# A written order for every engine through the first fourteen steps of an attention and feed-forward kernel, with the raw weights staged whole

## The chip, the cores and the metric

The kernel runs on one core of a Trainium2 chip. Five engines work side by side, each through its own list of instructions in order: TensorE (PE in the profile; its weight loads are PEld), VectorE (DVE), ScalarE (ACT), GpSimd (POOL) and SyncE (SP), which here only issues transfers. They meet through semaphores. The metric is the device time of one execution in microseconds (us); lower is better.

## The reference, cut to what matters

```python
# q, k, v: (4, 8, 768, 64); block = 32, window = 16, scale = 1/8, nb = 24
k_sum = k.reshape(B, H, nb, block, D).max(axis=3)        # 24 key summaries
v_sum = v.reshape(B, H, nb, block, D).mean(axis=3)       # 24 value summaries
scores_l = where(|i - j| < window, scale * q @ k.T, -1e9)
scores_s = scale * q @ k_sum.T + log(block)
a = softmax(concat(scores_l, scores_s), eps=1e-9)        # local keys, then summaries
x = a @ concat(v, v_sum)                                 # -> (3072, 512)
h = x @ w_in                                             # (3072, 2048)
g = (a0 + a1*h + a2*h*h + a3*h*h*h) / (1 + |b0|*|h| + |b1|*h*h + 1e-6)
out = g @ w_out                                          # (3072, 512)
```

The weights arrive as 64-bit floats and everything else as 32-bit ones.

## The kernel before, in words

**Attention** goes by "halves" of 64 queries, all eight heads at once; there are 48, twelve to a batch. A half sees 96 local keys and 24 summaries, so 120 columns for each of four head pairs. `att_a` makes the scores on PE, adds the mask and takes the row minimum on DVE (`tensor_tensor_reduce`, L195), the exponential with its row sum on ACT (L199), the small addition and the reciprocal on DVE (L201, L202), and scales the rows on POOL (L204). `att_b` turns the rows over on PE (L222) and copies them out of PSUM on ACT (L228). `att_c` multiplies with the values (for group 0 it also splits the result into a high and a low part, L252 and L253); `values` does two halves at once for the later groups.

**Feed-forward** goes by six groups of 512 tokens and sixteen chunks of 128 hidden columns: 96 steps. A step is twelve matmuls of the first layer (`moe1`), the rational function on ACT, DVE and POOL (`gelu`, L340 to L351), and, for the chunk three steps back (`LAG`), twelve matmuls of the second layer (`moe2`), with the transposes of a half between them. Three matmuls stand for one because each operand is split into a high and a low part.

**Weights.** Each of the sixteen chunks is loaded raw (1 MB), turned from a 64-bit float into a 32-bit one (ACT L314, POOL L316, DVE L317), copied as the high part (ACT L320) and subtracted for the low part (DVE L321). The first eight chunks come as one transfer each into a four-deep buffer; the last eight come as two transfers of 512 KB into the two-deep buffer `stage`, which the raw keys and values of later batches also use. `w_split` of chunk `fc` is traced five steps ahead (`CVL`).

**Start.** Group 0 needs its eight halves before the first step can begin. In that stage the kernel also makes the value summaries of batch 0 and of batch 1 by matmul (L154) and, where the planner puts them, splits of the first weight chunks.

**Order.** PE keeps the order of the text from the first step on (`chained`). DVE, ACT, POOL and the transfers are ordered by a planner that simulates a timeline and reads priorities (`high_priority`); only a few reductions on DVE are held in program order. `start_of` puts the halves of group 1 at steps 1, 2, 4, 5, 7, 8, 10 and 12.

Of the kernel before, what the change touches and what calls it, by code (L numbers as in the profile page):

```python
# [8 lines left out]
F32 = mybir.dt.float32  # L9
# [6 lines left out]
PSUM = bass.MemoryType.PSUM  # L16

# [25 lines left out]
CVL = 5  # L43
NEARLY = 3
SOFF = 12
VLAG = 5
NWARM = 6
FIRST = "Q0 K0 K1 V0 K2 K3 Q1 V1 S V2 W0 V3 F W1 V4 W2 G W3 V5"
AVGAT = 4
# [10 lines left out]
def tile_kernel(ctx, tc, qw_in, kraw, kwin, vpad, vred, wio, a, b, cmask, cident, cavg, out):  # L60
# [6 lines left out]
    wl = ctx.enter_context(tc.tile_pool(name="wl", bufs=NLATE))  # L67
# [7 lines left out]
    chained = []  # L75

    def mm(*args, **kw):
        ins = nc.tensor.matmul(*args, **kw)  # L78
        if chained:
            tc.keep_in_program_order(ins)  # L80
# [58 lines left out]
    def value_sum(bi, c):  # L139
        vs, vr = vsum[bi], sums.pop(("v", bi, c))  # L140
        tc.keep_in_program_order(nc.vector.tensor_reduce(vs[:, c, :], vr, axis=AX.X, op=ALU.add))
        if c == NVC - 1:
            nc.vector.tensor_scalar_mul(vs, vs, 1.0 / BLK)
# [9 lines left out]
    def value_average(bi, av, vt, i):  # L153
        nc.tensor.matmul(av[:NK, :], avg[:, AVGW - NK - 4 * i:AVGW - 4 * i], vt[i], start=(i == 0), stop=(i == len(vt) - 1))  # L154
        if i < len(vt) - 1:
            return
        if bi == 0:
            for i in range(2):
                nc.scalar.copy(vw[i][NKW:NK, :], av[NKW:NK, :])
            for t in vres[2:6]:  # L160
                nc.scalar.copy(t[NKW:NK, :], av[NKW:NK, :])
        else:
            t = gp.tile([NK, DM], F32, tag="gh", name="vn")
            nc.scalar.copy(t[NKW:NK, :], av[NKW:NK, :])
            nc.sync.dma_start(out=vnext, in_=t[NKW:NK, :])
# [9 lines left out]
    def att_a(jj, pool=None, tag="a", sbuf=None):  # L175
        bi, j = divmod(jj, NJ)
        kt, qt = kw[jj % 2], qw[jj % 2] if jj >= HPG else qres[:, jj]
        if j < 2 and bi > 0 or jj in (HPG, HPG + 1):
            nc.vector.tensor_copy(kt[:, NKC - 1], ksum[bi])
        mt = mask[:, 0 if j == 0 else (2 if j == NJ - 1 else 1), :]  # L180
        sc = (pool or ps_a).tile([P, 512], F32, tag=tag, name=f"sc{jj}")
        for pr in range(NPAIR):
            if jj >= HPG:
                parts = ((0, NK, kt[:, :, pr, :]),)
            else:
                parts = ((0, NKW, kres[:, pr, j * HQ:j * HQ + NKW]), (NKW, NK, ksum[0][:, pr, :]))
            for lo, hi, keys in parts:
                for e in range(2):
                    rows = slice(e * D, (e + 1) * D)
                    mm(sc[rows, pr * NK + lo:pr * NK + hi], qt[rows, pr, :], keys[rows], start=True, stop=True)  # L190
        sbuf, stag = sbuf or (pp, "p")
        ss = sbuf.tile([P, NPAIR, NK], F32, tag=stag, name=f"ss{jj}")
        sm = sp.tile([P, 2, NPAIR], F32, tag="sm", name=f"sm{jj}")
        for pr in range(NPAIR):
            nc.vector.tensor_tensor_reduce(  # L195
                out=ss[:, pr, :], in0=sc[:, pr * NK:(pr + 1) * NK], in1=mt, op0=ALU.add, op1=ALU.min,
                scale=-SCALE, scalar=3.0e38, accum_out=sm[:, 0, pr:pr + 1])
        for pr in range(NPAIR):
# [351 lines left out]
```

## Time and profile before

| | us |
|---|---|
| median of three runs | 695.42 (694.64 to 698.84) |
| profiled execution | 697.02 |
| its span, first to last instruction | 695.2 |
| first step begins (first matmul of the first layer) | 58.64 |
| step 14 begins | 168.32 |
| PE busy in the span | 662.9 |
| DVE busy in the span | 582.4 |
| ACT busy in the span | 472.0 |
| POOL busy in the span | 278.3 |

Times in the profile count from the first instruction of the span. A group line gives an instruction's line in the kernel, its engine and operation, what it writes and reads, how often it ran, its busy time, the mean of one in ns, and the idle time of the engine ahead of it with the engine that ended it. A timeline line begins with start and duration. A line of stretches gives the length, and then for each engine the busy time and the number of instructions, the granted TensorE clock as a share of full speed, the share of the DMA engines, and GB/s.

### The profile page before, as it was taken

The page shows a single profiled execution, that of the slowest core. Times are in us where ns is not written, and L with a number is a line of the kernel's source. Part 1 is how long each engine was busy: PE and PEld are TensorE (multiplying, and loading weights), DVE is VectorE, ACT ScalarE, POOL GpSimd, SP SyncE. Part 2 cuts the span into 40 slices and gives each one's busy share as a digit, 9 for nine tenths or more (in the row PEclk, how much of TensorE's full clock was granted, in tenths as well). Part 3 has the DMA queues.
Part 4 walks back from the last instruction along what each step waited for, and adds up shares of the span by engine and source line. Part 5 has one row for each costly group of instructions (what it writes and reads, how often), then busy time and mean ns, then how long its engine had stood idle before and what let it go on. Part 6 is the DMA issues. An engine that isn't in the chain of part 4 may idle for free.

```text
span 695.2 us, 11943 instructions
## 1 busy us (share of the span) xinstructions
PE 662.9 (95%) x4196; PEld 525.8 (76%) x4196; DVE 582.4 (84%) x1173; ACT 472.0 (68%) x1041; POOL 278.3 (40%) x320
## 2 busy tenths in 40 slices
PE   8887788988999999999999999999999999999997
PEld 4556566766888888888888888888888887888886
DVE  4567988878979998978879998888888888988885
ACT  2896766866785675785675776676785666665653
POOL 0670545755642443552442533442542442222221
PEclk9897999999999999999999999999999999999999
DMA  9991254342332330130122340111031000010001
GB/s 284 378 354 44 84 178 130 128 147 87 93 123 66 110 128 25 44 122 24 38 61 77 96 148 28 40 61 34 27 123 36 27 24 1 0 62 1 0 2 60
DMA packets 30680, 60.76 MB, mean 87 GB/s; under 512 B 3748, under 2 KB 15396, under 8 KB 29596
## 3 DMA queue, kind: packets, MB, share of 16 engines
q1 hardware_dynamic: 29916, 59.54, 26.2%
q8 instruction: 33, 0.54, 0.3%
q10 hardware_dynamic: 576, 0.25, 0.1%
q14 instruction: 27, 0.22, 0.1%
q0 software_dynamic: 128, 0.20, 0.1%
HBM read 53.44 MB, written 6.34 MB: 86 GB/s over the span
## 4 chain that ended last, share of the span: by engine, by line
PE 82%; DMA 5%; POOL 4%; DVE 4%; ACT 3%; issue 2%; SPq 0%; POOLq 0%; DVEq 0%; ACTq 0%
PE po L78 37%; PE h L78 34%; PE sc L78 5%; DMA wr<-in_wio_dram 4%; PE pt L222 3%; PE av L78 3%; POOL ss L204 2%; PE vf L154 1%; ACT ss L199 1%; DMA kres<-in_kraw_dram 1%; POOL wr L316 1%; DVE wr L317 1%; ACT wr L314 1%; POOL gl L351 1%; DMA qres<-in_qw_dram 0%
## 5 line engine op out<-in xcount | busy, mean ns | idle before, releaser
L351 POOL TENSOR_TENSOR gl<-tu,ta 128x512 fp32r<-128x512 f32 x96 | 131.4, 1369 | 284.9 <-DVE tu L350 152.9
L204 POOL TENSOR_SCALAR ss<-ss,sm 128x120 f32<-128x120 f32 x192 | 121.1, 647 | 90.1 <-DVE sm L202 65.2
L343 DVE SCALAR_TENSOR_TENSOR tq<-tq,cs,ta 128x512 f32<-128x512 f32 x96 | 108.2, 1127 | 35.4 <-ACT ta L341 34.8
L340 ACT ACTIVATE tq<-h 128x512 f32<-128x512 f32 x96 | 57.3, 597 | 116.1 <-PE h L78 115.2
L78 PE MATMUL po<-wearly,gh 128*128 128x512 f32 x384 | 129.0, 417 | 0.0
L78 PE MATMUL po<-w,gh 128*128 128x512 f32 x384 | 128.8, 417 | 0.0
L344 ACT ACTIVATE ta<-tq,cs 128x512 f32<-128x512 f32 x96 | 69.7, 726 | 54.1 <-DVE tq L343 53.6
L78 PE MATMUL h<-xh,wearly 128*128 128x512 f32 x384 | 97.3, 396 | 1.0 <-ACT xh L252 1.0
L78 PE MATMUL h<-xh,w 128*128 128x512 f32 x384 | 95.3, 390 | 0.0
L348 DVE SCALAR_TENSOR_TENSOR gh<-tu,cs,ta 128x512 fp32r<-128x512 f32 x96 | 76.2, 793 | 20.6 <-ACT ta L345 15.5
L78 PEld LDWEIGHTS h<-xh,wearly 128*128 128x128 f32 x384 | 73.0, 191 | 17.1 <-ACT xh L252 1.2
L78 PEld LDWEIGHTS h<-xh,w 128*128 128x128 f32 x384 | 72.4, 188 | 15.7
L199 ACT ACTIVATE ss<-ss,sm 128x120 f32<-128x120 f32 x192 | 73.5, 387 | 12.5 <-DVE sm L195 11.5
L78 PEld LDWEIGHTS po<-w,gh 128*128 128x128 f32 x384 | 67.0, 192 | 17.0 <-issue 2.1
L78 PEld LDWEIGHTS po<-wearly,gh 128*128 128x128 f32 x384 | 65.8, 191 | 16.5 <-issue 2.0
L78 PE MATMUL po<-w,gl 128*128 128x512 f32 x192 | 76.5, 398 | 0.0
L78 PE MATMUL po<-wearly,gl 128*128 128x512 f32 x192 | 75.8, 395 | 0.0
L342 ACT ACTIVATE tu<-h,cs 128x512 f32<-128x512 f32 x96 | 74.9, 780 | 0.0
L350 DVE SCALAR_TENSOR_TENSOR tu<-tu,cs,tq 128x512 f32<-128x512 f32 x96 | 72.4, 754 | 2.4
L347 DVE SCALAR_TENSOR_TENSOR tu<-tu,cs,h 128x512 f32<-128x512 f32 x96 | 71.6, 746 | 2.5
L222 PE MATMUL pt<-ident,ss 128*120 128x128 f32 x192 | 52.0, 284 | 18.9 <-POOL ss L204 18.8
L349 DVE SCALAR_TENSOR_TENSOR tq<-tq,gh 128x512 f32<-128x512 f32 x96 | 67.4, 702 | 2.5
(64 smaller groups left out, 1000.0 us busy)
## 6 DMA issues: line engine op xcount, KB each, us to landing
vw<-in_vpad_dram SPq DMA_DIRECT2D x44, 192.0 KB, 2.7
wr<-in_wio_dram SPq DMA_DIRECT2D x8, 1024.0 KB, 11.5
wr<-in_wio_dram SPq DMA_DIRECT2D x16, 512.0 KB, 4.2
kw<-in_kwin_dram SPq DMA_DIRECT2D x40, 192.0 KB, 3.4
out_dram<-o SPq DMA_DIRECT2D x24, 256.0 KB, 2.1
qw<-in_qw_dram SPq DMA_DIRECT2D x40, 128.0 KB, 3.0
kr<-in_kraw_dram SPq DMA_DIRECT2D x12, 384.0 KB, 3.6
vr<-in_vred_dram SPq DMA_DIRECT2D x8, 384.0 KB, 3.3
```

Of the source, the lines that this page charges most:

```text
L78: ins = nc.tensor.matmul(*args, **kw)
L199: nc.scalar.activation(ss[:, pr, :], ss[:, pr, :], AF.Exp, scale=-1.0, bias=sm[:, 0, pr:pr + 1], accum_out=sm[:, 1, pr:pr + 1])
L204: nc.gpsimd.tensor_scalar(ss[:, pr, :], ss[:, pr, :], sm[:, 1, pr:pr + 1], 1.0, op0=ALU.mult, op1=ALU.mult)
L222: ins = nc.tensor.transpose(out=pt[:NK, pr * P:(pr + 1) * P], in_=ss[:, pr, :], identity=ident)
L342: nc.scalar.activation(tu, h, AF.Identity, scale=cs[:, 3:4], bias=cs[:, 2:3])
L343: nc.vector.scalar_tensor_tensor(out=tq, in0=tq, scalar=cs[:, 5:6], in1=ta, op0=ALU.mult, op1=ALU.add)
L344: nc.scalar.activation(ta, tq, AF.Ln, bias=cs[:, 7:8])
L347: nc.vector.scalar_tensor_tensor(out=tu, in0=tu, scalar=cs[:, 1:2], in1=h, op0=ALU.add, op1=ALU.mult)
L348: nc.vector.scalar_tensor_tensor(out=gh, in0=tu, scalar=cs[:, 0:1], in1=ta, op0=ALU.add, op1=ALU.mult)
L349: nc.vector.scalar_tensor_tensor(out=tq, in0=tq, scalar=C1 * SH, in1=gh, op0=ALU.add, op1=ALU.mult)
L350: nc.vector.scalar_tensor_tensor(out=tu, in0=tu, scalar=cs[:, 0:1], in1=tq, op0=ALU.add, op1=ALU.subtract)
L351: nc.gpsimd.tensor_tensor(gl, tu, ta, op=ALU.mult)
```

## The change

A wrapper, `Kept`, stands between the text and each engine. While an engine is in `strict`, each of its instructions gets an ordering edge (no semaphore) to the one before it, so that the planner can't reorder it. PE is strict to the end; DVE, ACT and POOL are strict from the first half to the end of step 13 (`NSTRICT = NFC - 2`). The transfers on SyncE stay with the planner.

So that one engine's work can be put between another's, each routine becomes a generator that stops after each engine's part, and two strings give the order. `EARLY` orders the start: `s` scores and minimum of a half, `e` exponential to scaling, `v` a matmul of the value summaries, `p`/`P` transposes and their copy (on ACT, or on DVE for `P`), `c` values and split, `w` the next part of a weight chunk, `m` the copies of the summaries, `k` a copy of key summaries. `STEP` orders each of steps 0 to 13: `g` and `q` the rational function, `h` a half, `w` a weight chunk, `l` and `a` loads, `u` reductions and their loads, `P` the second layer with transposes, `v` the summaries of batch 1; the number says how many steps back (for `w`, ahead) the object lies.

Other parts: the small addition to the row sums goes from DVE (L201) to ACT, for all 48 halves. All raw chunks but the last are loaded in one transfer into a buffer of four named slots, and a slot's next load is issued when its chunk is done. The start holds weight chunks 0 and 1 whole and the first two parts of chunk 2; the rest are spread over steps 0 to 13. The summaries of batch 1 move from the start to steps 0 to 2. The copies of the first summaries go three times on ACT and five times on POOL (before: six on ACT). The last two halves' values get a tile of their own. Group 1's halves start at steps 0, 1, 3, 4, 6, 7, 9 and 10.

```diff
-FIRST = "Q0 K0 K1 V0 K2 K3 Q1 V1 S V2 W0 V3 F W1 V4 W2 G W3 V5"
-AVGAT = 4
+FIRST = "K0 Q0 K1 K2 K3 S F Q1 W0 V0 V1 V2 V3 V4 V5 V6 V7 W1 A8 A9 W2 W3 G"
+EARLY = ("s0 s1 e0 s2 e1 s3 v0 v1 s4 e2 e3 p0 v2 v3 s5 e4 P1 s6 v4 v5 w0 w0 e5 w0 P2 m0 s7 w0 w0 c0 e6 c1 P3 e7 p4 c2 p5 P6 c3 P7 k8 w1 w1 c5 c4 w1 c7 k9 c6 w1 w1 w2 w2")
...
+EARLY_HALF = (0, 1, 3, 4, 6, 7, 9, 10)
+NSTRICT = NFC - 2
+STEP = "h3 k0 h0 l0 a0 g1 h1 w2 h1 g1 h3 h0 g0 q0 w2 u g0 q0 w3 g1 h0 w2 w3 P2 v h2"
...
+            def call(*args, **kw):
+                traced = nc.cur_bb.bb.instructions
+                n = len(traced)
+                out = getattr(self.engine, name)(*args, **kw)
+                for ins in nc.cur_bb.bb.instructions[n:]:
+                    if ins.engine == out.ins.engine:
+                        if self.last is not None:
+                            tc.add_manual_dep(ins, self.last, ORDERED, reason="order of the text")
+                        if self in strict:
+                            self.last = ins.name
+                return out
...
-        nc.vector.tensor_scalar_add(sm[:, 1, :], sm[:, 1, :], 1e-9)
-        nc.vector.reciprocal(sm[:, 1, :], sm[:, 1, :])
+        act.activation(sm[:, 1, :], sm[:, 1, :], AF.Copy, bias=1e-9)
+        yield
+        dve.reciprocal(sm[:, 1, :], sm[:, 1, :])
...
+    def first_means(av):
+        for t in vres[0:3]:
+            act.copy(t[NKW:NK, :], av[NKW:NK, :])
+        for t in vres[3:]:
+            gps.tensor_copy(t[NKW:NK, :], vw[0][NKW:NK, :])
...
     def w_load(fc):
+        if fc == NFC - 1:
+            raws[fc] = [(slice(s, s + 1), stage.tile([P, 1, words], kind, tag="st", name=f"wr{fc}_{s}")) for s in range(2)]
+        else:
+            k = fc % NLATE if fc < NFC - NLATE else fc - (NFC - NLATE) + 1
+            raws[fc] = [(slice(0, 2), wl.tile([P, 2, words], kind, tag=f"wl{k}", name=f"wr{fc}"))]
+        for s, raw in raws[fc]:
+            nc.sync.dma_start(out=raw, in_=wio[fc, :, s, :].bitcast(kind))
...
+        for s, w, *_ in cooked:
+            dve.tensor_tensor(wt[:, 1, s, :], w, wt[:, 0, s, :], op=ALU.subtract)
+        ahead = fc + NLATE if fc < NFC - 2 * NLATE else fc + NLATE - 1
+        if fc != NFC - 2 * NLATE and ahead < NFC:
+            w_load(ahead)
...
+    strict |= {pe, dve, act, gps}
+
+    def lead(chain, all_of=False):
+        for _ in chain or ():
+            if not all_of:
+                return
...
+        strictly = step < NSTRICT
+        if step == NSTRICT:
+            strict -= {dve, act, gps}
...
+        for what in STEP.split() if strictly else ():
+            kind, n = what[0], int(what[1:] or 0)
+            if kind == "g":
+                lead(gelus.get(step - n))
+            elif kind == "q":
+                lead(prods.get(step - n))
+            elif kind == "h":
+                for jj in halves.get(step - n, ()):
+                    lead(chains.setdefault(("h", jj), whole(jj)))
...
+            elif kind == "w" and fc + n < NFC and g == 0:
+                lead(chains.setdefault(("w", fc + n), w_split(fc + n)))
...
+            elif kind == "P":
+                pt = (z for jj in halves.get(step - n, ()) for z in turned(jj))
+                po = second_layer(step, queue, po, pt)
+                lead(pt, True)
```

More of the change, by code (lines that the diff above doesn't have):

```diff
@@ L151, in value_tiles, with value_average, second_means @@
         return vt
[L153 to L165, printed above, removed]
+    def value_average(av, vt, i):
+        pe.matmul(av[:NK, :], avg[:, AVGW - NK - 4 * i:AVGW - 4 * i], vt[i], start=(i == 0), stop=(i == len(vt) - 1))
+    def first_means(av):
[3 more added lines that the diff above has]
+            gps.tensor_copy(t[NKW:NK, :], vw[0][NKW:NK, :])
+    def second_means(av):
+        t = pp.tile([NK, DM], F32, tag="p", name="vn")
+        act.copy(t[NKW:NK, :], av[NKW:NK, :])
+        nc.sync.dma_start(out=vnext, in_=t[NKW:NK, :])
     def first_q(lo, hi):
@@ L396, in tile_kernel @@
         elif what[0] == "W":
[L397 removed]
+            w_load(n)
         else:
             load_v(n)
[L400 to L414 removed]
@@ L456, in tile_kernel, with finish_half @@
[L456 to L461 removed]
+    strict |= {pe, dve, act, gps}
[3 more added lines that the diff above has]
+                return
+    def finish_half(jj, early, copy=None):
+        lead(turned(jj, early), True)
+        return values(jj, early, copy)
@@ new lines, in turned_copied, with whole @@
+    def turned_copied(jj):
+        yield from turned(jj)
+        copied(jj)
+    def whole(jj):
+        yield from scores(jj)
+        yield
+        yield from values(jj)
+    chains = {}
+    for what in EARLY.split():
+        kind, n = what[0], int(what[1:])
+        if kind == "s":
+            chains["a", n] = scores(n, True)
+            lead(chains["a", n])
+            lead(chains["a", n])
+        elif kind == "e":
+            lead(chains.pop(("a", n)), True)
+        elif kind in "pP":
+            chains["c", n] = finish_half(n, True, dve.tensor_copy if kind == "P" else None)
+            lead(chains["c", n])
+        elif kind == "v":
+            if n == 0:
+                vf = ps_a.tile([P, DM], F32, tag="a", name="vf")
+            value_average(vf, fv, n)
+        elif kind == "m":
+            first_means(vf)
+        elif kind == "k":
+            key_blocks(n)
+        elif kind == "w":
+            lead(chains.setdefault(("w", n), w_split(n)))
+        else:
+            lead(chains.pop(("c", n)), True)
@@ L462, in tile_kernel @@
+    def start_of(jj):
+        return EARLY_HALF[jj - HPG] if jj < 2 * HPG else NFC - 2 + 4 * ((jj - 2 * HPG) // 2)
+    halves = {}
+    for jj in range(HPG, NHALF):
+        halves.setdefault(start_of(jj), []).append(jj)
+    reduces, loads = {}, {}
     for bi in range(1, B):
@@ new lines, in tile_kernel @@
+        if strictly:
+            continue
+        if step in gelus:
+            with tc.high_priority(offset=-15):
+                lead(gelus.pop(step), True)
+        with tc.high_priority(offset=40):
+            if step - 4 >= NFC - 2 and halves.get(step - 4):
+                both_values(halves[step - 4][0])
+            for jj in halves.get(step, ()):
+                key_blocks(jj)
+                lead(scores(jj), True)
+            for jj in halves.get(step, ()):
+                load_v(jj)
+                if jj + 2 < NHALF:
+                    att_load(jj + 2)
@@ L496, in _layout @@
+        pt = (z for k in range(2) for jj in halves.get(step - 2 - k, ())[k:k + 1] if jj >= 2 * HPG for z in turned_copied(jj))
+        po = second_layer(step, queue, po, pt)
+        with tc.high_priority(offset=40):
+            lead(pt, True)
+        for f, *args in reduces.get(step, []) + loads.get(step, []):
+            f(*args)
 def _layout(q, k, v, moe_w_in, moe_w_out, moe_a, moe_b):
```

355 lines of the change are left out of this document (166 added, 189 removed).

## The prediction

> **What bounds the kernel now.** I read the page's summary and its chain first, then the stretches of time, then the groups of the first 168 us.
>
> ```profile
> span 695.2 us, 11943 instructions
> ...
> PE   8887788988999999999999999999999999999997
> ...
> PEclk9897999999999999999999999999999999999999
> ...
> PE 82%; DMA 5%; POOL 4%; DVE 4%; ACT 3%; issue 2%; SPq 0%; POOLq 0%; DVEq 0%; ACTq 0%
> ```
>
> PE carries the chain, and its gaps and its low clock lie in the first ten of 40 slices. Two rows of the timeline mark the first step and step 14; the stretches between them follow.
>
> ```profile
> 58.64 3.78 PE L78 MATMUL h<-xh,wearly 128*128 128x512 f32 x8 [1.00 <-ACT xh L252]
> 168.32 2.02 PE L78 MATMUL h<-xh,w 128*128 128x512 f32 x8
> ```
>
> ```profile
> 0.00:58.60 58.60, 45.73 (x452) 28.63 (x452) 35.51 (x113) 39.71 (x103) 27.36 (x44) 0.86 0.89 305
> 58.60:168.30 109.70, 94.06 (x556) 71.45 (x557) 92.17 (x198) 77.34 (x176) 58.57 (x61) 0.94 0.38 122
> 0.00:168.30 168.30, 139.79 (x1008) 100.09 (x1009) 127.68 (x310) 117.05 (x279) 85.93 (x105) 0.91 0.56 186
> 168.30:695.20 526.90, 523.07 (x3189) 425.75 (x3187) 454.72 (x863) 354.95 (x763) 192.35 (x216) 1.00 0.18 56
> ```
>
> After 168.3 PE is busy for 523.1 of 526.9 us at full clock: that tail is PE's own work, and the change leaves the work in it alone (one pair of value products, about 1 us, moves ahead of it). So the time is the moment at which step 14 begins, plus 526.9, plus the 1.8 that the profiled execution (697.0) has outside its span. Up to there PE idles for 28.5 us and works below full clock; neither PE nor any other engine is full in the start (58.6), and in the 109.7 us of steps 0 to 13 DVE has 92.2, or 84%, and PE 94.1 with part of it at low clock.
>
> **The start.** What the change takes out of it are six of the eight weight chunks split there and the summaries of batch 1.
>
> ```profile
> L204 POOL TENSOR_SCALAR ss<-ss,sm 128x120 f32<-128x120 f32 x32 | 17.0, 550 | 17.4 <-DVE sm L202 16.5 <-DVE sm L195 0.6
> L199 ACT ACTIVATE ss<-ss,sm 128x120 f32<-128x120 f32 x32 | 12.3, 396 | 10.2 <-DVE sm L195 10.2
> L317 DVE SCALAR_TENSOR_TENSOR wr<-wr 128x1024 int32<-128x1024 int32 x8 | 10.7, 1334 | 9.8 <-POOL wr L316 9.8
> L316 POOL TENSOR_SCALAR wr<-wr 128x1024 int32<-128x1024 uint8 x8 | 10.1, 1264 | 10.0 <-DMA wr<-in_wio_dram 9.8
> L321 DVE TENSOR_TENSOR wearly<-wr,wearly 128x1024 fp32r<-128x1024 f32 x7 | 9.8, 1401 | 3.0 <-ACT wearly L320 2.9
> L314 ACT ACTIVATE wr<-wr 128x1024 f32<-128x1024 f32 x8 | 9.4, 1173 | 3.8 <-DMA wr<-in_wio_dram 3.8
> L320 ACT CAST wearly<-wr 128x1024 fp32r<-128x1024 f32 x7 | 8.0, 1145 | 2.9 <-DVE wr L317 2.9
> L199 ACT ACTIVATION_READ_ACCUMULATOR ss<-ss,sm 128x1 f32 x32 | 6.4, 200 | 0.0
> L228 ACT COPY pts<-pt 120x512 f32<-120x512 f32 x8 | 4.6, 593 | 0.0
> L252 ACT CAST xh<-av 128x256 fp32r<-128x256 f32 x8 | 3.1, 390 | 1.2 <-PE av L78 1.2
> L161 ACT COPY vr<-vf 24x512 f32<-24x512 f32 x4 | 2.0, 580 | 0.0
> L201 DVE TENSOR_SCALAR sm<-sm 128x4 f32<-128x4 f32 x8 | 1.4, 173 | 2.7 <-ACT ss L199 2.5
> ```
>
> These are the groups of the start. Before, 17 us of ACT (9.4 + 8.0), 20 of DVE (10.7 + 9.8) and 10 of POOL went into weights there. Three more rows give where ACT and POOL begin and PE's second pass of summaries:
>
> ```profile
> 12.04 0.40 ACT L199 ACTIVATE ss<-ss,sm 128x120 f32<-128x120 f32 x1 [10.01 <-DVE sm L195]
> 14.26 1.39 POOL L204 TENSOR_SCALAR ss<-ss,sm 128x120 f32<-128x120 f32 x4 [13.81 <-DVE sm L202]
> 37.90 5.41 PE L154 MATMUL vf<-vf,kres 128*120 128x512 f32 x12
> ```
>
> ACT's list up to the first step, by the new order: exponentials 12.3, with their readings nearly beneath them; eight small additions at 0.2 (by the reading, the nearest row with so few columns; 0.4 if they cost what 120 columns do) 1.6; three copies of turned tiles 1.8; three of summaries 1.7; chunk 0 whole 2.3, the first part of chunk 1 1.2; eight casts 3.1. That is 24.0, from 12.04 to 36.0. POOL: scalings 17.0, one chunk 1.3, and five copies of summaries, which no row shows. They lie between the 0.55 of a 120-column scaling and the 1.26 of a 1024-column conversion; I take 0.85, the mean of the 512-column conversion quoted below, 4.3 in all. That is 22.6, from 14.26 to 36.9. So POOL ends last, and behind it the last half still has its transposes, copy, values and two splits:
>
> ```profile
> 43.73 0.65 PE L222 MATMUL pt<-ident,ss 128*120 128x128 f32 x4
> ...
> 45.16 0.80 PE L78 MATMUL av<-pts,vr 120*64 120x64 f32 x18
> ```
>
> ```profile
> L369 DVE COPY o<-po 128x512 f32<-128x512 f32 x2 | 1.4, 692 | 3.5 <-PE po L78 3.5
> ```
>
> 0.65 + 0.69 (the copy of this half moves to DVE) + 0.80 + 0.39 + 0.4 is 2.9: 39.8. With about a microsecond for the hand-overs the first step begins at 41, against 58.6. The ends are 38 (ACT's sum and the tail's splits, POOL's copies cheap) and 45 (copies at 1.26 and two waits in a row). Data don't hold it:
>
> ```profile
> 0.00:20.00 20.00, 14.79 (x162) 9.25 (x162) 9.36 (x40) 6.64 (x25) 3.67 (x10) 1.00 0.93 293
> 20.00:40.00 20.00, 19.48 (x175) 12.12 (x176) 12.63 (x56) 17.59 (x47) 12.52 (x22) 0.83 1.04 379
> ```
>
> Keys 1.6 MB, queries 1.0, values 1.5 twice, constants 0.3 and two chunks 2.0 make 7.9 MB; at 293 and then 379 GB/s they are there at 25 us, in the order in which the text asks for them. Six requests are moved ahead to here: values 6 and 7, counted above, and two halves' keys and queries, 0.6 MB, which delay only chunk 2, to 30 by the same rate.
>
> **Steps 0 to 13.** DVE's work up to step 14 was 127.7. Five copies of turned tiles come to it (3.5), sixteen small additions leave (16 x 0.173 = 2.8): 128.4. The start now holds 35.5 - 20.5 + 5.5 (two chunks) + 3.5 - 1.4 + 0.4 = 23.0 of it, so the steps hold 105.4. The next rows are groups of these steps:
>
> ```profile
> L348 DVE SCALAR_TENSOR_TENSOR gh<-tu,cs,ta 128x512 fp32r<-128x512 f32 x13 | 13.1, 1007 | 2.8 <-ACT ta L345 2.6
> L317 DVE SCALAR_TENSOR_TENSOR wr<-wr 128x512 int32<-128x512 int32 x14 | 10.2, 728 | 6.1 <-POOL wr L316 6.1
> L314 ACT ACTIVATE wr<-wr 128x512 f32<-128x512 f32 x14 | 9.5, 682 | 5.3 <-DMA wr<-in_wio_dram 5.2
> L204 POOL TENSOR_SCALAR ss<-ss,sm 128x120 f32<-128x120 f32 x32 | 24.7, 788 | 8.3 <-DVE sm L202 5.3 <-ACT ta L345 2.8
> L316 POOL TENSOR_SCALAR wr<-wr 128x512 int32<-128x512 uint8 x16 | 13.6, 852 | 15.9 <-DMA wr<-in_wio_dram 7.3 <-DVE kw L179 2.4 <-DVE sm L202 2.0
> ```
>
> Fourteen of the sixteen half-chunks were through DVE before; the new order finishes the last too, 2.7 more: 108.1, or 7.7 a step. PE can begin step 14 while DVE still has one step to do (two PSUM buffers hold `h`), so 100.4 must be done. To that come 3 for the first step, in which DVE waits for the first `h`, and stalls. DVE's idle time was 17.5 of 109.7; 6.1 of it stood behind weights whose transfer was late (the three rows that end in DMA or POOL `wr`), and four whole slots give a transfer three steps. I take 6 for the rest: 109. PE's own work, 94.1 and the 5.4 of batch 1's summaries, is 7.1 a step and stays under DVE's 7.7; were PE the longer, that pass would cost its 5.4. The new wait in ACT's list is the copy of a turned half behind the step's transposes; queued behind it are the logarithm and exponential for which DVE's L348 waits. As PE runs ahead it should cost nothing, and the 6 covers it if not.
>
> The addition on ACT: nearest rows 0.2 and 0.4, so 3.2 to 6.3 in all on an engine that was busy for 77.3 where DVE was for 92.2. The Trainium skill (ScalarE: Activation LUTs, Rules for kernel authors) says to give additions to VectorE; by that rule the 2.8 would stay on DVE and the time would be 682, and the two engines' shares here speak against it. For the other 32 halves PE's full tail hides either.
>
> **Sum.** 41 + 109 = 150; 150 + 526.9 + 1.8 = 679 against the profiled 697.0. The median of the runs is 1.6 lower than that; I leave these 1.6 for DVE's lag in steps 14 and 15, and forecast 679. Its own ends: 38 + 102 gives 669, less the 1 of the moved pair 668; 45 + 113 gives 687.
>
> **The rivals.** *Work only moved.* DVE stays at 84% in the steps, because what held it were hand-overs and not the order; that also covers edges that only repeat the planner's order. 105.4 / 0.84 is 125.5; 41 + 125.5 = 166.5, so 695: nothing gained. For it: of 17.5 idle only 6.1 is named by weights.
>
> *Contention.* POOL's scaling took 0.79 in the steps and 0.55 in the start, and L348 1.01 where its mean over the whole run is lower:
>
> ```profile
> L348 DVE SCALAR_TENSOR_TENSOR gh<-tu,cs,ta 128x512 fp32r<-128x512 f32 x96 | 76.2, 793 | 20.6 <-ACT ta L345 15.5
> ```
>
> If a denser order puts both engines' work on top of each other, the start pays 32 x 0.24 = 7.6 and the steps once more 14 x 0.21 = 3: 690. The Trainium skill (GPSIMD Engine Reference, 1. Specifications) says so: POOL shares its SBUF interfaces with VectorE, whose instructions with two SBUF inputs contend. The rows agree; against a full price speaks that POOL has less to do in the new start.
>
> *A late weight in a fixed order.* ACT now can't pass over a chunk that hasn't landed.
>
> ```profile
> SPq L210 <- PE av L78: 270.1, 21, 22.7
> ...
> wr<-in_wio_dram SPq DMA_DIRECT2D x8, 1024.0 KB, 11.5
> ```
>
> A slot is held from the first part to the subtraction, some 1.25 steps or 10 us; landing takes 11.5; and the request waits behind others on SP, above all loads of values. Four steps must hold these: 31 us, so the wait decides from 9.7. At the longest wait seen, 22.7, a step takes 44.2 / 4 = 11.05; over ten steps that is 32 more: 711, slower than before. Against it: the text asks for values only just behind the product that frees them.
>
> **Chances.** Forecast 0.65, work only moved 0.12, contention 0.10, late weight 0.13. About 1% is what can be told from no change here: 688.5 and 702.4. Faster 0.65; within 0.22 (two rivals); slower 0.13. The range goes from the forecast's low end, 668, past 695 to 697; it leaves out the late weight and little else.
>
> **What would show it.** The first matmul of `h` near 41 with ACT and POOL nearly full from 14 on; step 14 near 150; DVE above 90% between them; idle behind DMA `wr` gone; the tail again 527. Wrong would be: a first step after 47 (POOL's groups then show why), steps of 8.5 or more with DVE idle behind ACT or PE (work only moved), ACT's L314 part waiting for DMA (late weight), or a PE that idles after step 14.

## The result

The changed kernel takes 674.88 us (median of 4 runs, 672.82 to 676.86) where the kernel before takes 695.53 (694.64 to 698.84): a ratio of 0.9694, with a 95% interval of 0.9651 to 0.9737. The forecast was 679, from 668 to 697. The profiled execution took 674.83 with a span of 673.0. In the changed kernel every instruction passes through the wrapper, so almost all its rows carry one line number, L85; the names of the tiles tell them apart.

The page's summary of the kernel after: the span, PE's busy tenths and granted clock in 40 slices, and the engines' shares of the chain of waits.

```profile
span 673.0 us, 11873 instructions
...
PE   8897989998999999999999999999999999999997
...
PEclk9988989999999999999999999999999999999999
...
PE 82%; DVE 8%; DMA 3%; ACT 3%; issue 2%; POOL 1%; SPq 0%; DVEq 0%; ACTq 0%
```

POOL's share of the chain has gone from 4% to 1%, DVE's has doubled from 4% to 8%. The timeline of the kernel after, first the first step and then step 14; the columns are start and duration:

```profile
40.57 2.11 PE L85 MATMUL h<-xh,wearly 128*128 128x512 f32 x8 [0.47 <-ACT xh L85]
144.27 1.98 PE L85 MATMUL h<-xh,w 128*128 128x512 f32 x8
```

The stretches of the kernel after: length, then busy time and count of PE, PEld, DVE, ACT and POOL, the granted clock, the DMA share and GB/s.

```profile
0.00:40.60 40.60, 35.35 (x441) 24.43 (x441) 22.67 (x99) 24.26 (x91) 20.73 (x45) 0.92 0.99 327
40.60:144.30 103.70, 97.05 (x601) 73.79 (x602) 100.87 (x182) 90.48 (x185) 62.31 (x57) 0.95 0.52 177
144.30:673.00 528.70, 522.78 (x3157) 424.52 (x3155) 451.41 (x837) 358.92 (x794) 180.60 (x217) 1.00 0.17 55
```

The start is 18.0 us shorter (58.6 to 40.6), the steps 0 to 13 are 6.0 shorter (109.7 to 103.7), and the tail is 1.8 longer (526.9 to 528.7): 22.2 of the span's 695.2. In the steps DVE is now busy for 100.87 of 103.70 us, or 97%, where it was at 84%. What is left of its waits there, from the view of DVE's waits between 40.6 and 144.3 us of the kernel after (total, times, longest):

```profile
DVE ss L85 <- PE sc L85: 0.7, 1, 0.7
DVE sm L85 <- ACT sm L85: 0.7, 1, 0.7
DVE wearly L85 <- ACT wearly L85: 0.6, 1, 0.6
```

The 6.1 us that stood behind weights before are gone: in steps 0 to 13 no engine waits for a transfer of `wr`.

### The profile page after: what moved, and what is told of

Its sections match the earlier page's. It is cut to its first block, busy times and chain, and to the rows that moved or that the text cites. A ratio compares the mean times of both kernels' runs of the same rounds, so it can differ in the third digit from the quotient of the medians.

```text
span 673.0 us, 11873 instructions
## 1 busy us (share of the span) xinstructions
PE 655.2 (97%) x4196; PEld 522.7 (78%) x4196; DVE 574.9 (85%) x1116; ACT 473.7 (70%) x1068; POOL 263.6 (39%) x318
## 4 chain that ended last, share of the span: by engine, by line
PE 82%; DVE 8%; DMA 3%; ACT 3%; issue 2%; POOL 1%; SPq 0%; DVEq 0%; ACTq 0%
PE po L85 36%; PE h L85 34%; PE sc L85 6%; PE av L85 3%; PE pt L85 3%; DVE tu L85 2%; DMA wr<-in_wio_dram 2%; DVE tq L85 2%; DMA kres<-in_kraw_dram 1%; DVE wr L85 1%; DVE gh L85 1%; PE vf L85 1%; ACT ta L85 1%; ACT ss L85 1%; DVE w L85 1%
## 5 line engine op out<-in xcount | busy, mean ns | idle before, releaser
L85 POOL TENSOR_TENSOR gl<-tu,ta 128x512 fp32r<-128x512 f32 x96 | 128.3, 1337 | 289.9 <-DVE tu L85 159.9
L85 POOL TENSOR_SCALAR ss<-ss,sm 128x120 f32<-128x120 f32 x192 | 107.1, 579 | 101.5 <-DVE sm L85 101.3
L85 DVE SCALAR_TENSOR_TENSOR tq<-tq,cs,ta 128x512 f32<-128x512 f32 x96 | 106.3, 1107 | 38.9 <-ACT ta L85 38.3
L85 ACT ACTIVATE tq<-h 128x512 f32<-128x512 f32 x96 | 57.2, 596 | 107.1 <-PE h L85 104.3
L85 PE MATMUL po<-wearly,gh 128*128 128x512 f32 x384 | 130.2, 421 | 0.0
L85 PE MATMUL po<-w,gh 128*128 128x512 f32 x384 | 126.7, 411 | 0.0
L85 ACT ACTIVATE ta<-tq,cs 128x512 f32<-128x512 f32 x96 | 69.7, 726 | 50.0 <-DVE tq L85 49.5
L85 PE MATMUL h<-xh,wearly 128*128 128x512 f32 x384 | 96.8, 393 | 1.7 <-DVE tu L85 1.1
L85 PE MATMUL h<-xh,w 128*128 128x512 f32 x384 | 95.1, 390 | 0.0
L85 DVE SCALAR_TENSOR_TENSOR gh<-tu,cs,ta 128x512 fp32r<-128x512 f32 x96 | 77.5, 807 | 18.5 <-ACT ta L85 9.9
L85 PEld LDWEIGHTS h<-xh,wearly 128*128 128x128 f32 x384 | 71.7, 188 | 19.9 <-DVE tu L85 1.6
L85 PEld LDWEIGHTS h<-xh,w 128*128 128x128 f32 x384 | 72.1, 188 | 15.5
L85 ACT ACTIVATE ss<-ss,sm 128x120 f32<-128x120 f32 x192 | 73.3, 386 | 10.8 <-DVE sm L85 10.0
L85 PEld LDWEIGHTS po<-wearly,gh 128*128 128x128 f32 x384 | 66.4, 193 | 17.7 <-issue 2.6
L85 PEld LDWEIGHTS po<-w,gh 128*128 128x128 f32 x384 | 65.9, 189 | 16.9 <-issue 1.3
L85 PE MATMUL po<-w,gl 128*128 128x512 f32 x192 | 75.4, 392 | 1.0 <-POOL gl L85 1.0
L85 PE MATMUL po<-wearly,gl 128*128 128x512 f32 x192 | 76.2, 397 | 0.0
L85 ACT ACTIVATE tu<-h,cs 128x512 f32<-128x512 f32 x96 | 74.9, 781 | 0.0
L85 DVE SCALAR_TENSOR_TENSOR tu<-tu,cs,tq 128x512 f32<-128x512 f32 x96 | 72.0, 750 | 2.7
L85 DVE SCALAR_TENSOR_TENSOR tu<-tu,cs,h 128x512 f32<-128x512 f32 x96 | 71.4, 744 | 2.2
L85 DVE SCALAR_TENSOR_TENSOR tq<-tq,gh 128x512 f32<-128x512 f32 x96 | 66.6, 694 | 3.2
L85 ACT ACTIVATE ta<-h,cs 128x512 f32<-128x512 f32 x96 | 65.5, 682 | 4.2 <-POOL gl L85 4.2
```

The lines of the kernel that those rows point to most:

```text
L85: out = getattr(self.engine, name)(*args, **kw)
```

## The experiments

Each is an edit of the changed kernel, and each time stands beside runs of the kernel before on the same chip; the ratios are to that kernel. "First step" and "step 14" are the starts of those matmuls in each profiled execution.

### The order alone, and its two halves

First the written order of DVE, ACT and POOL was taken out, with all else kept: PE alone keeps the order of the text.

```diff
-    strict |= {pe, dve, act, gps}
+    strict |= {pe}
```

> The changed kernel with its text, loads and staging, but only TensorE held to the order of the text; VectorE, ScalarE and GpSimd are ordered by the planner again. Theory (the fixed order is what keeps VectorE at 97% in steps 0 to 13): VectorE falls back towards the 84% of before, 100.9 us of work take about 117 instead of 103.7, and the planner pulls some weight work into the start again; 688 us (682 to 695). Rival (fewer weights in the start and whole staging are the gain, the order adds nothing): 675, within 2.

Measured: 696.14 (694.91 to 697.67), ratio 1.0015 [1.0000, 1.0029]. The stretches of this kernel before and after its first step:

```profile
0.00:58.00 58.00, 41.20 (x441) 29.85 (x441) 34.16 (x108) 37.09 (x102) 29.99 (x49) 0.74 0.88 300
58.00:167.80 109.80, 100.12 (x600) 74.17 (x601) 95.37 (x183) 81.03 (x178) 55.11 (x54) 0.93 0.40 137
```

The time lies 1 us above the range of the theory and 21 above the rival. These are the lengths of the kernel before (58.6 and 109.7). Whole staging, the addition on ACT, the moved summaries and the earlier halves bring nothing without the order, and what the text moves out of the start the planner took back: the text asks for 2 weight chunks and a part of a third there, the planner put 8 (group of ACT in 0 to 58 us):

```profile
L85 ACT ACTIVATE wr<-wr 128x1024 f32<-128x1024 f32 x8 | 9.3, 1158 | 4.6 <-DMA wr<-in_wio_dram 4.4
```

The next two split the order in time. One keeps it in the start only, by freeing the three engines just ahead of the loop over the steps:

```diff
+    strict -= {dve, act, gps}
```

> The changed kernel with VectorE, ScalarE and GpSimd held to the text in the start alone; from the first step on the planner orders them. Theory (the order kept the six weight chunks out of the start; in the steps it keeps VectorE full): the first step still at 40.6, then the planner's 87% (95.4 of 109.8 in the run with its order throughout) with all of the 100.9 us of work: 116, step 14 near 157, in all 687 (683 to 691). Rival (the start's order is the whole gain): 675 to 678.

Measured: 696.89 (692.99 to 699.24), ratio 1.0019 [0.9994, 1.0043]. First step 40.65, as in the changed kernel; then this stretch:

```profile
40.65:169.20 128.55, 103.92 (x600) 76.66 (x601) 108.98 (x192) 93.78 (x190) 62.89 (x58) 0.89 0.42 148
```

All 17 us of the start are given back, and the time lies 6 us above the theory's range: the steps take 128.6, with DVE at 85%. This is the prediction's rival "work only moved", whose 125.5 us at 84% lies about 3 from it; it happens where the steps are left to the planner. DVE's work itself is 8 us more than with the order (108.98 against 100.87). Counted by groups, some 7 of these are more instructions, not longer ones: each of the six operations of the rational function ran once more before step 14 (the one from `tu` and `h` 14 times, against 13), and the last chunk's two halves were subtracted too. The theory had put 100.9 there.

The other keeps it in the steps only, by putting the three engines in `strict` just ahead of the loop over the steps:

```diff
-    strict |= {pe, dve, act, gps}
+    strict |= {pe}
...
+    strict |= {dve, act, gps}
```

> The changed kernel with VectorE, ScalarE and GpSimd held to the text in steps 0 to 13 alone; the start is the planner's. Theory (a weight chunk that has its place in the steps' order can't be pulled ahead): the start holds two chunks and a part and ends between 41 and 46, the steps take 104: 675 to 681. Rival (the start needs its own order, hand by hand): first step near 58, and as the chunks are still to do in the steps, 692 or more.

Measured: 682.79 (682.13 to 683.29), ratio 0.9821 [0.9783, 0.9859], a little above the range of the theory and far below the rival's 692.

```profile
0.00:48.10 48.10, 36.02 (x441) 24.52 (x441) 24.85 (x101) 26.51 (x92) 22.16 (x45) 0.89 0.91 315
48.10:151.90 103.80, 97.04 (x600) 73.77 (x601) 98.50 (x180) 88.29 (x183) 62.32 (x57) 0.95 0.47 159
```

The steps are as short as in the changed kernel (103.8), and the first step comes at 48.1. ACT begins three weight chunks in this start, not eight. So the first step moves from 58.0 to 48.1 because the order of the steps keeps weight chunks out of the start, and from 48.1 to 40.6 by the start's own order. By the medians: 696.1 with neither, 696.9 with the start's alone, 682.8 with the steps' alone, 674.9 with both. The start's order is worth 8 us, but only if the steps are ordered too.

### The place of the weights

Here chunks 1 to 3 are split ahead of the last halves' values, by the string of the start alone (the same parts, moved):

```diff
-EARLY = ("... w0 w0 c0 e6 c1 P3 e7 p4 c2 p5 P6 c3 P7 k8 w1 w1 c5 c4 w1 c7 k9 c6 w1 w1 w2 w2")
+EARLY = ("... w0 w0 w1 w1 w1 w1 w1 w2 w2 w2 w2 w2 w3 w3 w3 w3 w3 c0 e6 c1 P3 e7 p4 c2 p5 P6 c3 P7 k8 c5 c4 c7 k9 c6")
```

> The changed kernel with chunks 1 to 3 split whole in the start, ahead of the values; steps 0 to 13 keep chunks 4 to 15. Theory (VectorE's work up to step 14 is a fixed sum, and where it lies counts only by idle time): the start grows by about 5 to 7 us, from 40.6 to 46 or 47, the steps lose 4.9 of VectorE's work and stop at TensorE's 97: step 14 at 145, in all 675 to 678. Rival (the shorter start is the gain by itself): 680 to 682. Other rival (the start has that much idle time): 671.

Measured: 690.04 (689.11 to 691.31), ratio 0.9930 [0.9911, 0.9949]. First step 55.42, not 46 to 47. The stretches of this kernel:

```profile
28.00:43.00 15.00, 0.67 (x7) 0.42 (x4) 7.79 (x6) 6.34 (x6) 8.05 (x8) 0.59 1.04 362
...
55.40:155.80 100.40, 94.00 (x600) 71.95 (x601) 94.95 (x177) 85.32 (x180) 60.51 (x57) 0.98 0.44 144
```

Adding up one engine's work was the wrong sum. From 28 to 43 us PE does 0.67 us of work and no other engine is more than 54% busy: written out one behind the other, a chunk goes POOL, DVE, ACT, DVE, each waiting for the last, as the timeline shows where ACT and DVE take turns (the bracket holds the idle time ahead and who ended it):

```profile
34.21 1.10 ACT L85 CAST wearly<-wr 128x1024 fp32r<-128x1024 f32 x1 [4.66 <-DVE wr L85]
...
35.34 2.03 DVE L85 TENSOR_TENSOR wearly<-wr,wearly 128x1024 fp32r<-128x1024 f32 x1 [1.17 <-ACT wearly L85]
37.30 1.21 DVE L85 SCALAR_TENSOR_TENSOR wr<-wr 128x1024 int32<-128x1024 int32 x1
38.55 1.11 ACT L85 CAST wearly<-wr 128x1024 fp32r<-128x1024 f32 x1 [2.23 <-DVE wr L85]
```

In these 15 us ACT's waits for DVE add up to 8.2 us, DVE's for ACT to 2.3 and its one wait for POOL, which copies the summaries first, to 3.9; late data are only 0.7 of it. The start is 14.9 us longer, the steps are only 3.3 shorter for it (100.4), the tail is 3.1 longer, where PE once waits 3.1 us for GpSimd's `gl`, and the end comes 15 us later. A written order is not good as such: it fixes hand-overs too, and a list should alternate two chains so that each hides the other's waits, as the string of the changed kernel does.

### The staging

The late chunks come in two transfers through the two-deep buffer again, asked for at their split, while the order stays:

```diff
     def w_load(fc):
-        if fc == NFC - 1:
+        if fc >= NSTG:
...
+        if fc >= NSTG:
+            w_load(fc)
...
-        ahead = fc + NLATE if fc < NFC - 2 * NLATE else fc + NLATE - 1
-        if fc != NFC - 2 * NLATE and ahead < NFC:
-            w_load(ahead)
+        if fc + NLATE < NSTG:
+            w_load(fc + NLATE)
```

> The changed kernel with chunks 8 to 15 loaded as before the change, in two transfers of 512 KB into the two-deep buffer, each requested when the buffer comes free; the order of the text stays fixed. Theory (a fixed order needs its weights in time): ScalarE now waits in line for each of these chunks, a step of 5 to 12 takes 10 us held and 5 to 8 us landing instead of 7.2, so 20 to 60 us more: 695 to 735. Rival (the staging is beside the point): 675, within 2.

Measured: 726.30 (723.67 to 728.34), ratio 1.0448 [1.0422, 1.0475], with the first step at 40.26. The waits of ACT from 40 to 200 us in this kernel:

```profile
ACT wr L85 <- DMA wr<-in_wio_dram: 54.5, 14, 8.6
```

The time lies in the range of the theory (695 to 735). Step 14 begins at 197.66, so the steps are 53.7 us longer, about what ACT waits. This is the prediction's slower rival at work, with its place and its kind of price: ACT can't pass over a chunk that hasn't landed, and everything that it owes the step waits too. In the changed kernel this wait does not occur at all, so the new staging is what makes the order bearable. The edit takes back both the depth of the buffer and the early request, and the run doesn't tell the two apart. The two parts of the change need each other: staging without order gives nothing (696), and order without this staging is 31 us slower than the kernel before.

### The small addition

```diff
-        act.activation(sm[:, 1, :], sm[:, 1, :], AF.Copy, bias=1e-9)
         yield
+        dve.tensor_scalar_add(sm[:, 1, :], sm[:, 1, :], 1e-9)
```

> The changed kernel with the small addition back on VectorE, for all 48 halves. Theory (VectorE's sum sets the length of steps 0 to 13): eight additions of 0.17 us come to a full VectorE there, 1.4 us more, nothing in the start or behind step 14: 676.3, within 1. Rival (ScalarE is the worse place, as a hand-over and 0.2 us on its list): 673 to 674.

Measured: 676.03 (675.75 to 680.96), ratio 0.9741 [0.9714, 0.9769]; first step 40.84, step 14 at 145.28, 1.0 later than in the changed kernel. It points the expected way, by 1.1 us, but the intervals overlap with those of the changed kernel. On ACT the addition takes this (group of the start of the kernel after):

```profile
L85 ACT ACTIVATE sm<-sm 128x4 f32<-128x4 f32 x8 | 1.6, 206 | 0.3
```

0.206 us, the 0.2 of the prediction. The rule of the Trainium skill (ScalarE: Activation LUTs, Rules for kernel authors), additions to VectorE, finds no support here. One addition is a little shorter on DVE (173 ns in the start before), but the kernel with all of them on DVE was not faster; a difference of 1 us is too small to say more.

### What holds the steps now

If DVE alone set the steps' length, less work on it would shorten them by as much. Two products of the rational function are left out in steps 0 to 13:

```diff
-            dve.tensor_tensor(tu, tu, h, op=ALU.mult)
+            if g or fc >= NSTRICT:
+                dve.tensor_tensor(tu, tu, h, op=ALU.mult)
...
-            dve.scalar_tensor_tensor(out=tu, in0=tu, scalar=cs[:, 1:2], in1=h, op0=ALU.add, op1=ALU.mult)
+            if g or fc >= NSTRICT:
+                dve.scalar_tensor_tensor(out=tu, in0=tu, scalar=cs[:, 1:2], in1=h, op0=ALU.add, op1=ALU.mult)
```

> The changed kernel without the two products of the rational function on VectorE in steps 0 to 13 (its result there is another one): 14 times 1.27, 17.8 us of VectorE's work less. Theory (VectorE's sum is the bound of these steps, TensorE's 97 us the next one): the steps go from 103.7 to 97 to 99, in all 668 to 670. Rival (hand-overs between the engines set the pace, not a sum): 673 to 675. Other rival (nothing else is near): 657.

Measured: 672.76 (671.97 to 673.74), ratio 0.9678 [0.9640, 0.9715]: some 2 us less, where 5 to 7 were expected, and a little below the first rival's 673 to 675. The steps' stretch and three DVE groups in it, first of this kernel:

```profile
39.80:140.50 100.70, 95.17 (x600) 72.98 (x601) 94.35 (x158) 92.14 (x186) 64.88 (x57) 0.97 0.54 182
```

```profile
L85 DVE TENSOR_TENSOR w<-wr,w 128x1024 fp32r<-128x1024 f32 x7 | 15.4, 2201 | 0.0
L85 DVE SCALAR_TENSOR_TENSOR tq<-tq,cs,ta 128x512 f32<-128x512 f32 x13 | 15.3, 1176 | 0.0
L85 DVE TENSOR_TENSOR wearly<-wr,wearly 128x1024 fp32r<-128x1024 f32 x7 | 11.5, 1637 | 0.8 <-ACT wearly L85 0.8
```

and then the same groups of the changed kernel, with one that reads `h` from PSUM:

```profile
L85 DVE SCALAR_TENSOR_TENSOR tq<-tq,cs,ta 128x512 f32<-128x512 f32 x13 | 14.9, 1145 | 0.0
L85 DVE TENSOR_TENSOR w<-wr,w 128x1024 fp32r<-128x1024 f32 x7 | 10.1, 1447 | 0.0
L85 DVE SCALAR_TENSOR_TENSOR tu<-tu,cs,h 128x512 f32<-128x512 f32 x13 | 9.6, 737 | 0.0
L85 DVE SCALAR_TENSOR_TENSOR gh<-tu,cs,ta 128x512 fp32r<-128x512 f32 x12 | 9.2, 765 | 0.0
L85 DVE TENSOR_TENSOR wearly<-wr,wearly 128x1024 fp32r<-128x1024 f32 x7 | 9.0, 1291 | 0.6 <-ACT wearly L85 0.6
```

The two products' durations add up to 18.5 us (9.6 above, and 8.9 by the group of the other), but DVE's busy time fell by 6.5 only. Durations of neighbours overlap a little (two of DVE's at 95.4 us of the changed kernel by 0.08), so a sum of them says too much; but the subtractions of the weights alone took 7.8 us more, from 1447 to 2201 ns and from 1291 to 1637. The products read PSUM; with them gone more subtractions, whose inputs both lie in SBUF, begin while GpSimd is at work. The rows of a GpSimd instruction and of the subtraction beside it show this, first of the changed kernel (a weight conversion, `wr`), then of this one, and last a subtraction of the changed kernel with nothing of GpSimd beside it:

```profile
95.67 1.50 POOL L85 TENSOR_SCALAR wr<-wr 128x1024 int32<-128x1024 uint8 x1
96.76 1.49 DVE L85 TENSOR_TENSOR w<-wr,w 128x1024 fp32r<-128x1024 f32 x1
```

```profile
92.42 1.43 POOL L85 TENSOR_SCALAR wr<-wr 128x1024 int32<-128x1024 uint8 x1
92.81 2.12 DVE L85 TENSOR_TENSOR w<-wr,w 128x1024 fp32r<-128x1024 f32 x1
```

```profile
72.95 1.21 DVE L85 TENSOR_TENSOR wearly<-wr,wearly 128x1024 fp32r<-128x1024 f32 x1
```

So it goes for all fourteen in the steps. In the changed kernel five have nothing beside them (1.21 to 1.23 us), eight begin about 1.05 us after a conversion (1.47 to 1.50), and one begins just ahead of a conversion (1.21). In this kernel four have nothing beside them (1.21 to 1.23), six begin 0.4 us after a conversion (2.11 to 2.14) and four 0.4 to 0.5 us after GpSimd's product `gl` (2.30 to 2.32).

PE (95.2) and ACT (92.1) are now about as full as DVE (94.4) in these 100.7 us, and DVE's idle time went from 2.8 to 6.4 us, so hand-overs have a part in it too. With three engines level, it is likely that none of them alone gives much; no run shows it. The tail is 1.3 us longer than in the changed kernel.

Whether GpSimd's product is what lengthens DVE's work was asked directly, with DVE's own work kept. GpSimd's product with two inputs is replaced by a copy of one, in the same place:

```diff
-        gps.tensor_tensor(gl, tu, ta, op=ALU.mult)
+        if g == 0 and fc < NSTRICT:
+            gps.tensor_copy(gl, tu)
+        else:
+            gps.tensor_tensor(gl, tu, ta, op=ALU.mult)
```

> The changed kernel with GpSimd's product of the low part replaced by a copy of one of its two inputs for chunks 0 to 13 of group 0 (the factor is left out there); 14 of GpSimd's two-input instructions less. Theory (it is this product that holds VectorE up: 1.15 for the denominator's sum instead of 0.75, 1.29 to 1.45 for the weights' subtraction instead of 1.22): the sum at 0.75 to 0.9, VectorE's busy time in steps 0 to 13 down from 100.9 to 95 to 97, the steps from 103.7 to 99 to 101, in all 670 to 672.5. Rival (VectorE is slowed by its own reads of two inputs and by anything on GpSimd alike): unchanged, 673.5 to 676.

Measured: 669.85 (669.70 to 671.45), ratio 0.9628 [0.9595, 0.9662], 5.0 us less than the changed kernel and just below the theory's range. Stretches and groups of this kernel:

```profile
39.70:141.60 101.90, 96.82 (x601) 73.95 (x602) 99.35 (x185) 91.08 (x186) 52.84 (x57) 0.95 0.53 180
```

```profile
L85 DVE SCALAR_TENSOR_TENSOR tq<-tq,cs,ta 128x512 f32<-128x512 f32 x13 | 14.2, 1092 | 0.0
...
L85 DVE TENSOR_TENSOR w<-wr,w 128x1024 fp32r<-128x1024 f32 x7 | 9.0, 1288 | 0.0
```

```profile
L85 POOL CAST gl<-tu 128x512 fp32r<-128x512 f32 x12 | 7.3, 610 | 19.5 <-DVE tu L85 15.0 <-PE po L85 4.5
```

In the changed kernel the same stretch has these two groups of GpSimd:

```profile
L85 POOL TENSOR_SCALAR ss<-ss,sm 128x120 f32<-128x120 f32 x32 | 29.3, 932 | 23.9 <-DVE sm L85 23.9
L85 POOL TENSOR_TENSOR gl<-tu,ta 128x512 fp32r<-128x512 f32 x12 | 15.5, 1289 | 18.3 <-DVE tu L85 13.7 <-ACT wr L85 4.7
```

GpSimd's part fell from 1289 to 610 ns, and DVE's groups with two SBUF inputs fell with it (1145 to 1092, 1447 to 1288), while the one that reads `h` stays at 737. But the time was hit without the mechanism that was named for it. The denominator's sum was to fall to 0.75 to 0.9 us and took 1.09; DVE's busy time was to fall to 95 to 97 us and fell to 99.35. The product is only a part of the cause: of the seven subtractions of `w` the two that still begin behind a weight conversion took 1.47 and 1.49 us and the other five 1.21, and of the eight sums above 1.1 us five began during a weight conversion (1.18 to 1.54) and three as the copy began (1.16).

Of the 5 us, 2.7 came before step 14, which begins at 141.57, and 2.2 behind it, where 526.5 us follow, not 528.7. In the changed kernel PE waits there for two results, in the first 32 us after step 14:

```profile
PE h L85 <- DVE tu L85: 1.1, 1, 1.1
PE po L85 <- POOL gl L85: 1.0, 1, 1.0
```

With the copy neither wait occurs. The copy has one input and is also half as long; which of the two counts is open. The Trainium skill (SBUF — State Buffer, Who interferes with whom) says that a VectorE instruction with two SBUF inputs contends with a GpSimd instruction that reads SBUF, and one with at most one SBUF input doesn't, outside its two-port modes. The rows agree for GpSimd's product and weight conversion, where these were already running (1.47 to 2.32 us instead of 1.21), and for the operation that reads `h` from PSUM (0.73 to 0.75 beside either). GpSimd's scalings cost less or nothing: in the kernel before, the 128x512 subtractions with a scaling beside them took 657 to 684 ns, those without 684 to 689.

### Three attempts at a better version

The changed kernel as it is was run once more, on one chip with the second and the third, so that there is a second measurement of it; the first ran on another chip.

> The changed kernel itself, beside the next two on one chip: 674.9, within 1.

Measured: 674.94 (672.96 to 676.86), ratio 0.9704 [0.9672, 0.9736]; first step 39.59, step 14 at 144.31. So in two executions of the same kernel step 14 comes at the same time (144.27 and 144.31), while the first step differs by 1.0 and the steps by as much (103.7 and 104.7). The first attempt keeps PE busy in the start with ten matmuls that nobody reads, in a free PSUM bank:

```diff
-... e7 p4 c2 p5 P6 c3 P7 k8 ...
+... e7 p4 d2 c2 d4 p5 d2 P6 d2 c3 P7 k8 ...
...
+        elif kind == "d":
...
+            for _ in range(n):
+                pe.matmul(chains["keep"][:, 0:P], ident, ident, start=True, stop=True)
```

> The changed kernel with ten matmuls of the identity between the transposes and values of halves 2 to 6, into a PSUM bank that nobody reads. In the changed kernel TensorE's clock falls to half from 33.5 to 39.9 us, after waits of about a microsecond each. Theory (the start's end is TensorE's at half clock: 34.0 to 40.5 for work that takes half as long at full clock): full clock there, the first step at 38 to 39, in all 672 to 673.5. Rival (the end is copies and splits handed from engine to engine, the clock costs nothing): 675, or 676 with the matmuls in the way.

Measured: 673.78 (673.39 to 679.42), ratio 0.9711 [0.9670, 0.9752]. PE's clock from 28 to 42 us, of this kernel and then of the changed one:

```profile
28.00:42.00 14.00, 11.84 (x148) 9.62 (x145) 10.34 (x21) 10.13 (x31) 10.01 (x16) 1.00 1.04 366
```

```profile
28.00:42.00 14.00, 10.94 (x124) 8.78 (x123) 9.12 (x22) 9.79 (x32) 10.19 (x17) 0.76 1.04 354
```

The clock stays full and the first step comes at 39.20, but the unedited kernel's own start varies as much: its second profiled execution has a clock of 0.88 in these 14 us and the first step at 39.59. The times overlap as well: inconclusive. The second puts DVE's products that read PSUM ahead, where GpSimd's product runs:

```diff
-STEP = "... u g0 q0 w3 g1 h0 w2 w3 P2 v h2"
+STEP = "... u q0 g0 w3 g1 h0 w2 w3 P2 v h2"
```

> The changed kernel with one pair of letters exchanged in the order of a step: VectorE takes the second product of the rational function (which reads PSUM) ahead of the denominator's sum (two inputs from SBUF). In the changed kernel that sum takes 1.15 us in steps 0 to 13 where 0.75 is its length undisturbed, because GpSimd's product of the low part runs beside it. Theory (two SBUF inputs on VectorE stand still while GpSimd's two-input product runs): the sum falls to 0.75 to 0.9, 3 to 5 us of VectorE's time less, of which TensorE's 97 us leave 2 to 4: 671 to 673. Rival (a collision only moves to the next instruction with two SBUF inputs, or ScalarE waits longer for the later sum): 674 to 676.

Measured: 674.34 (674.06 to 678.88), ratio 0.9710 [0.9672, 0.9749]. The `tq` operation fell from 1145 to 1056 ns and the subtraction of `w` rose from 1447 to 1544; three of the seven began while a weight conversion ran and took 1.68 to 2.16 us. This is the rival: the collision moved to the next instruction with two SBUF inputs. The third has both edits:

> The exchanged letters and the ten matmuls that keep TensorE's clock together. Theory: both gains add, 1.2 from the start and 2 to 4 from the steps: 670 to 672. Rival: only the start's, 673.5 to 674.5.

Measured: 673.87 (673.63 to 678.56), ratio 0.9699 [0.9664, 0.9735]. Its trace is not like its median: in the profiled execution (678.56) DVE stands for 4.1 us in the start, at 19 to 23 us, with no wait that the profile shows, and the first step comes at 44.52; the steps (103.9) and the tail (528.4) are as long as without the edits. None of the three can be told from the changed kernel.

## Why the prediction was right, point by point

**The start: 41 forecast, 40.57 measured, with errors that cancel.** The groups of POOL in the start of the kernel after:

```profile
L85 POOL TENSOR_SCALAR ss<-ss,sm 128x120 f32<-128x120 f32 x32 | 12.1, 400 | 17.2 <-DVE sm L85 17.0
...
L85 POOL COPY vr<-vw 24x512 f32<-24x512 f32 x3 | 2.8, 972 | 0.1
L85 POOL COPY vlast<-vw 24x512 f32<-24x512 f32 x2 | 1.2, 612 | 0.0
```

The five copies that no row showed cost 4.0 against the 4.3 taken. The scalings cost 0.40 each and not the 0.55 of the start before, 4.9 us less in all; the prediction carried that 0.55 over. It also gave POOL's list no idle time, and between its scalings POOL waited 3.5 us for DVE. So POOL's last scaling ended at 34.96 and not at 36.9. But the work behind it took 5.6 us and not 2.9 with about 1 for hand-overs. PE ran at half clock there (stretches of the kernel after), which explains some 1.1 of it: with the ten matmuls, at full clock, the same work took 4.5 us, from 34.70 to 39.20.

```profile
28.00:30.00 2.00, 1.24 (x16) 1.00 (x16) 1.75 (x6) 1.96 (x10) 1.94 (x3) 1.00 1.12 424
30.00:32.00 2.00, 0.80 (x19) 0.69 (x16) 1.20 (x3) 1.98 (x10) 2.00 (x4) 1.00 0.98 404
32.00:33.00 1.00, 0.45 (x5) 0.23 (x3) 0.18 (x1) 0.97 (x5) 0.90 (x4) 1.00 1.04 434
33.00:34.00 1.00, 1.00 (x4) 0.46 (x3) 0.42 (x1) 0.47 (x1) 1.00 (x4) 0.52 0.91 369
```

The sum of POOL's list was no proof that POOL ends last, either: in 28 to 33 us ACT and POOL are both nearly full. That the errors add up to less than half a microsecond is luck.

**Steps 0 to 13: 109 forecast, 103.7 measured; the stalls are the term that was mis-sized.** DVE's work up to step 14 was put at 100.4, and DVE was busy for 100.87. Idle time was put at 3 for the first step and 6 for stalls, and 2.8 came. These 6 us are more than the 4 that the forecast is off; the tail gives 1.8 of them back. The order itself was what had been missing: the same text in the planner's hands leaves DVE idle for 14.4 of 109.8 us (no order) or 19.6 of 128.6 (start only). That DVE's sum came out within 0.5 us is partly luck too: inside it two shifts nearly cancel, `gh` at 765 ns where it took 1007 (2.9 us less for 12 of them), and `tq` at 1145 (4.3 more for 13), where the kernel before has this group in the steps:

```profile
L343 DVE SCALAR_TENSOR_TENSOR tq<-tq,cs,ta 128x512 f32<-128x512 f32 x14 | 11.4, 814 | 2.5 <-ACT ta L341 2.5
```

**PE under DVE.** It held, but narrowly: 97.05 of 103.70. Without the two products PE, ACT and DVE are level.

**The addition.** The prediction's sum with the additions left on DVE, 682, is too high by its own terms: only eight of the sixteen lie in the steps, so 1.4 us and not 2.8 would come back, which is 680. The experiment gave 1.1.

**The tail: 526.9 and 1.6 for DVE's lag forecast, 528.7 measured.** In the 31.7 us after step 14 PE is idle for 2.1, where the kernel before leaves it no gap. Half of it is the lag of DVE that the 1.6 was left for (1.1 us for `tu`), the other half one of GpSimd's product (1.0), which the prediction did not have; with GpSimd's copy the tail is 526.5. The prediction also took the median as 1.6 below the profiled execution; after the change the two agree (674.88 and 674.83), so that difference did not come back.

**The rivals.** *Work only moved* is what the planner makes of it in the steps: the experiment with the start's order alone gave 696.9, against the 695 worked out. (By the prediction's own 108.1 for all of DVE's work the steps would be 108.1 / 0.84 = 128.7, and 128.6 were measured.) It didn't come because the order reaches through step 13. *Contention* was there in kind but not at its price: the scalings in the steps rose from 0.79 to 0.93 us on an engine that is busy for 60% of them, and no run shows what that costs; `tq` paid 4.3 us and `gh` gave 2.9 back; and the start paid nothing. It is now one of the things that hold the steps: with GpSimd's product shortened step 14 comes 2.7 us earlier. *The late weight* is real for the two-deep buffer (726.3) and absent with four whole slots; the prediction's argument against it, that the text asks for values only just behind the product that frees them, was not tested by itself.

*What the prediction did not ask* is what its parts are worth alone. It gave the start and the steps a sum each; measured against the kernel before, the start's order alone gave nothing, the steps' alone 12 us, staging without order nothing, and order without the staging a loss.

## What to carry to other kernels

When a stage has no full engine and no late data, look at who sets the order, and fix it across the whole stretch in which the moved work lands; ordering only the stretch that you want shorter hands its gain to the next. Before fixing an order on in-order engines, make sure that everything that arrives from memory has a buffer of its own that is asked for early enough, and alternate two chains in the list, since a sum per engine says nothing of hand-overs in one chain. When the bound engine is 97% busy, look at its durations in the new company and not at the old ones, instruction by instruction: a group's mean hides which of them began behind another engine's work.

## What the runs showed of the hardware

Operations on VectorE with two inputs in SBUF vary with what GpSimd does as they begin: the subtraction of a 128x1024 tile took 1288, 1447 and 2201 ns on average in three kernels that differ in nothing of its own, while a product that reads PSUM stayed at 737 to 744. One by one, the subtraction took 1.21 to 1.23 us with nothing of GpSimd beside it and up to 2.32 where GpSimd's product or weight conversion was already running. Where it began 15 ns ahead of a conversion (142.60 in the changed kernel) it kept its 1.21 us, and the conversion of half a tile took 1.71, where the one before it took 0.98. A cure at one place moved the cost to another operation.

TensorE fell to half clock at 33 us after five microseconds in which it was busy for 2.5, in pieces (1.50 of the last 3.41); no single wait was longer than 1.20 us, as the timeline of PE in the kernel after shows:

```profile
31.69 0.62 PE L85 MATMUL pt<-ident,ss 128*120 128x128 f32 x4 [1.20 <-DVE pts L85]
32.86 1.26 PE L85 MATMUL pt<-ident,ss 128*120 128x128 f32 x4 [0.55 <-ACT pts L85]
```

The Trainium skill (TensorE: Matmul & The Clock Gate, What's actually happening) says that the clock falls after an idle window of about 3.4 us; here a half idle stretch was enough, and with ten matmuls in the gaps the clock stayed full in the one execution that was profiled.

GpSimd's 120-column scaling took 0.40 us in this start, 0.55 in the start before, and 0.93 in the steps: one operation on one engine, with a factor of more than two between its neighbourhoods.
